# Group normalization on one core: VectorE's scaling in a register loop, and no spacer loads

## The chip, the cores and the metric

The kernel runs on one core of one Trainium2 chip. The metric is the device time in microseconds (us) of one execution. Before the change the median of 3 runs is 633.09 us (632.92 to 633.27). The core has five instruction streams that meet only in semaphores: TensorE (PE in the profile), VectorE (DVE), ScalarE (ACT), GpSimd (POOL) and SyncE (SP), which here only issues DMAs. The DMAs run on 16 DMA engines.

## The reference

The input x has shape (128, 1024, 32, 16) in bfloat16, 134 MB; the output has the same shape. The 1024 channels fall into 32 groups of 32 channels. For each sample and group the mean and variance over 32 channels times 512 pixels (16,384 elements) are taken, and then each channel is scaled and shifted:

```python
xr = x.reshape(B, G, C // G, H, W)
mu = xr.mean(axis=(2, 3, 4), keepdims=True)
var = ((xr - mu) ** 2).mean(axis=(2, 3, 4), keepdims=True)
xn = (xr - mu) / jnp.sqrt(var + 1e-5)
return xn.reshape(B, C, H, W) * g[None, :, None, None] + b[None, :, None, None]
```

With one scale and one bias per (sample, group, channel) this is out = x * (rstd * g) + (b - mean * rstd * g).

## The kernel before

**Tiling.** A tile holds 4 samples times 32 groups on the 128 partitions; each partition has its 32 channels times 512 pixels, so a tile is 128 x 16,384 bfloat16, 4.19 MB, 32 KB of consecutive DRAM per partition. There are 32 tiles and 6 buffers `xt` (NBUF). Tile i lies in buffer (i + 4) % 6. A tile is loaded, worked on in place and stored from the same buffer.

**The stages of one tile.** SP loads it. TensorE adds up its 32 channels into one PSUM bank with 32 matmuls against the identity (L194). VectorE turns the bank into minus the mean with one accumulating pass of 512 elements (`mean`, L211). ScalarE squares the two halves of the tile with that bias and accumulates (L316), then makes the standard deviation (L330, L337). VectorE takes the reciprocal (L223), makes 32 scales (`scl`, L226) and 32 biases (`bia`, L233) and scales the tile, one instruction per channel, 32 of 128 x 512 (L243). The last of them raises `s_dve`, and SP stores the tile (L171).

**The order on VectorE** is the mean of tile i + 1 first, then the reciprocal, scales, biases and 32 scalings of tile i. So the scaling of a tile waits until the next tile has been loaded and summed.

**The loop.** PE, ACT and DVE each run a loop of 6 trips over the 6 buffers, entered at buffer 4 (`loop`, L95). The body of VectorE is written out for all 6 buffers, with constant addresses; at the end of a trip it waits once, sets three semaphore counts back, adds one to the trip's register and branches.

**SP's queue** sets the order of the DMAs. All go through one queue, which the DMA engines take in order. SP first issues 6 loads and one spacer, a load of 128 x 32 elements (64 bytes a partition) into a tile that nobody reads. Then it walks over the tiles: wait for `s_dve`, store. After the stores 1, 4, 7, ... 25 it issues three loads (two after store 1), each behind a wait until the store from that buffer has landed, and one more spacer:

```python
            if (NT - NBUF - 1 - i) % RUN == 0 and i < NT - NBUF:
                for n in range(max(NBUF, i + 1 + NBUF - RUN), min(i + 1 + NBUF, NT)):
                    load(n)
                spacer()
```

So the DMA engines see runs of three stores and three loads, and a spacer after each run of loads. A spacer waits until the spacer before it has landed. The last six stores follow without loads.

The lines below are those of the kernel before.

## Time and profile before

| What | Value |
|---|---|
| time, median of 3 runs | 633.09 us |
| the profiled execution: time / span | 633.13 us / 631.3 us |
| DMA: share of the 16 engines' span, mean rate | 99.0%, 425 GB/s |
| HBM read / written | 134.30 MB / 134.22 MB |
| ACT busy | 476.2 us (75%) |
| DVE busy | 375.8 us (60%), 1024 scalings L243 among 1188 instructions |
| PE busy | 255.1 us (40%) |
| spacers | 10, 8 KB each |

The span goes from the first to the last instruction of the profiled execution; its time is 1.8 us longer. The busy share of an engine is an average over a start, a steady stretch and an end. In the timeline an entry "x32" merges neighbouring instructions: its first number is the start, the second the length of the whole. The bracket behind an entry is the idle time of that engine just before it and what ended it; "issue" means that the profile shows nothing that was waited for. An entry of SPq is the issue of a DMA, not its transfer.

### The profile page before, as it was taken

The page shows a single profiled execution, that of the slowest core. Times are in us where ns is not written, and L with a number is a line of the kernel's source. Part 1 is how long each engine was busy: PE and PEld are TensorE (multiplying, and loading weights), DVE is VectorE, ACT ScalarE, POOL GpSimd, SP SyncE. Part 2 cuts the span into 40 slices and gives each one's busy share as a digit, 9 for nine tenths or more (in the row PEclk, how much of TensorE's full clock was granted, in tenths as well). Part 3 has the DMA queues.
Part 4 walks back from the last instruction along what each step waited for, and adds up shares of the span by engine and source line. Part 5 has one row for each costly group of instructions (what it writes and reads, how often), then busy time and mean ns, then how long its engine had stood idle before and what let it go on. Part 6 is the DMA issues. An engine that isn't in the chain of part 4 may idle for free. (4 is left out here: it accounts for less than half of the span.)

```text
span 631.3 us, 3704 instructions
## 1 busy us (share of the span) xinstructions
PE 255.1 (40%) x1009; PEld 105.4 (17%) x1025; DVE 375.8 (60%) x1188; ACT 476.2 (75%) x194; POOL 0.9 (0%) x7
## 2 busy tenths in 40 slices
PE   0967409009602750582087018404720770095000
PEld 0423103003201320230032003101300230032000
DVE  0057777774772777077727735770777177447771
ACT  0499999995994699189929965993899199649930
POOL 0000000000000000000000000000000000000000
PEclk9998858658855985687578659855975796598555
DMA  8999999999999999999999999999999999999996
GB/s 363 432 432 414 434 432 432 438 432 432 430 432 434 430 430 434 432 430 432 432 432 432 432 432 430 432 432 432 430 432 434 432 430 432 432 432 436 438 394 283
DMA packets 10756, 268.57 MB, mean 425 GB/s; under 512 B 2560, under 2 KB 2560, under 8 KB 2560
## 3 DMA queue, kind: packets, MB, share of 16 engines
q1 hardware_dynamic: 10656, 268.52, 99.0%
q10 hardware_dynamic: 96, 0.00, 0.0%
q14 instruction: 3, 0.02, 0.0%
q8 instruction: 1, 0.02, 0.0%
HBM read 134.30 MB, written 134.22 MB: 425 GB/s over the span
## 5 line engine op out<-in xcount | busy, mean ns | idle before, releaser
L316 ACT ACTIVATE ja<-xt,negmean 128x8192 fp8e5<-128x8192 bf16 x64 | 455.5, 7117 | 126.9 <-DVE jd L211 125.5
L194 PE MATMUL pa<-xt,eye 128*128 128x512 bf16 x1008 | 254.9, 414 | 312.4 <-PEq L192 310.9
L243 DVE TENSOR_SCALAR xt<-xt,scl,bia 128x512 bf16<-128x512 bf16 x1024 | 333.7, 408 | 1.2
L194 PEld LDWEIGHTS pa<-xt,eye 128*128 128x128 bf16 x1024 | 105.3, 105 | 461.6 <-issue 366.0
L211 DVE TENSOR_SCALAR_CACHE_REDUCE jd<-pa 128x512 bf16<-128x512 f32 x33 | 22.7, 687 | 147.3 <-PE pa L194 145.4
L223 DVE RECIPROCAL rstd<-std 128x1 f32<-128x1 f32 x32 | 5.2, 163 | 78.1 <-ACT std L337 78.1
L316 ACT ACTIVATION_READ_ACCUMULATOR ja<-xt,negmean 128x1 f32 x64 | 11.9, 186 | 0.0
L337 ACT ACTIVATE std<-sq,half 128x1 f32<-128x1 f32 x32 | 9.4, 295 | 1.0
L330 ACT ACTIVATE half<-sq,eps_t 128x1 f32<-128x1 f32 x32 | 8.9, 278 | 0.0
L233 DVE SCALAR_TENSOR_TENSOR bia<-scl,negmean,gb 128x32 f32<-128x32 f32 x32 | 8.1, 252 | 1.1
L226 DVE TENSOR_SCALAR scl<-gb,rstd 128x32 f32<-128x32 f32 x32 | 7.7, 241 | 1.1
L262 DVE COPY gb<-gb_p 128x64 f32<-128x64 f32 x1 | 0.2, 226 | 10.7 <-PE gb_p L181 10.7
L181 PE MATMUL gb_p<-gb_b,rep 32*128 32x64 bf16 x1 | 0.2, 231 | 12.5 <-DMA gb_b<-in_b_dram 12.5
L211 DVE DVE_READ_ACCUMULATOR jd<-pa 128x1 f32 x33 | 2.7, 83 | 0.0
L312 ACT ACT_TABLE_LOAD x1 | 1.3, 1283 | 1.9 <-issue 1.9
L181 PEld LDWEIGHTS gb_p<-gb_b,rep 32*128 32x128 bf16 x1 | 0.1, 100 | 12.5 <-DMA gb_b<-in_b_dram 12.5
L261 DVE MEMSET ones_b<- 128x128 bf16 x1 | 0.2, 165 | 1.9 <-issue 1.9
L289 POOL TENSOR_SCALAR_AFFINE_SELECT rep<-ones_b 32x128 bf16<-32x128 bf16 x1 | 0.3, 303 | 0.0
L280 POOL TENSOR_SCALAR_AFFINE_SELECT eye<-ones_b 128x128 bf16<-128x128 bf16 x1 | 0.3, 294 | 1.7 <-DVE ones_b L261 1.7
L312 ACT ACTIVATE warm<-eps_t 128x1 f32<-128x1 f32 x1 | 0.2, 203 | 0.0
L298 POOL TENSOR_SCALAR eps_t<-ones_b 128x1 f32<-128x1 bf16 x1 | 0.2, 205 | 0.0
L378 POOL MEMSET const-uint8-127<- 128x1 uint8 x1 | 0.1, 103 | 0.0
(3 smaller groups left out, 0.3 us busy)
## 6 DMA issues: line engine op xcount, KB each, us to landing
xt<-in_x_dram SPq DMA_DIRECT2D x32, 4096.0 KB, 29.1
out_dram<-xt SPq DMA_DIRECT2D x32, 4096.0 KB, 33.2
spare<-in_x_dram SPq DMA_DIRECT2D x10, 8.0 KB, 29.2
gb_b<-in_g_dram ACTq DMA_DIRECT2D x1, 2.0 KB, 7.8
gb_b<-in_b_dram ACTq DMA_DIRECT2D x1, 2.0 KB, 11.0
```

The lines of the kernel that those rows point to most:

```text
L181: pe.matmul(out=gb_p[:].rearrange("p a k -> p (a k)"), lhsT=rep[:], rhs=gb_b[:].rearrange("q a k -> q (a k)"), start=True, stop=True,).the ...
L194: m = pe.matmul(out=pa[j][:], lhsT=eye[:], rhs=xt[j][:, k * MM_FREE : (k + 1) * MM_FREE], start=(k == 0), stop=(k == NMM - 1),)
L211: dve.tensor_scalar(out=jd[j % 2][:], in0=pa[j % NBUF][:], scalar1=-inv_n, scalar2=None, op0=ALU.mult, op1=ALU.add, accum_out=col(negmean, j),
L223: dve.reciprocal(out=col(rstd, j), in_=col(std, j))._wait_ge(s_std, j + 1).then_inc(s_dd, 1)
L226: dve.tensor_scalar(out=scl[j][:], in0=gam, scalar1=col(rstd, j), scalar2=None, op0=ALU.mult,)._wait_ge(s_dd, 3 * j + 2).then_inc(s_dd, 1)
L233: dve.scalar_tensor_tensor(out=bia[j][:], in0=scl[j][:], scalar=col(negmean, j), in1=bet, op0=ALU.mult, op1=ALU.add,)._wait_ge(s_dd, 3 * j ...
L243: m = dve.tensor_scalar(out=span, in0=span, scalar1=scl[j][:, k : k + 1], scalar2=bia[j][:, k : k + 1], op0=ALU.mult, op1=ALU.add,)
L280: pool.affine_select(out=eye[:], in_=ones_b[:], pattern=[[-1, P]], compare_op=ALU.is_equal, fill=0.0, base=0, channel_multiplier=1,)._wait ...
L312: act.activation(out=warm[:], in_=eps_t[:], func=ACT.Sqrt)
L316: m = act.activation(out=ja[:], in_=xt[j][:, h * F // 2 : (h + 1) * F // 2], func=ACT.Square, bias=col(negmean, j), scale=1.0, accum_out=s ...
L330: act.activation(out=col(half, j), in_=sq[:, 2 * j : 2 * j + 1], func=ACT.Identity, bias=eps_t[:], scale=inv_n,)._wait_ge(s_sq, 3 * j + 1) ...
L337: act.activation(out=col(std, j), in_=sq[:, 2 * j + 1 : 2 * j + 2], func=ACT.Sqrt, bias=col(half, j), scale=inv_n,)._wait_ge(s_sq, 3 * j + ...
```

## The change

It has two parts.

**VectorE's loop.** The body written out for 6 buffers becomes a loop over the 32 tiles with the buffer's number `j` in a register. The six buffers become slices of one tile `x_all`, the PSUM banks slices of `pa_all`, and the addresses come from expressions of registers (`at`, with `bass.ds`). `scl`, `bia` and `rstd` have one copy instead of six. The 32 scalings become an inner loop of 4 rounds of 8 instructions; the addresses of the tile's span, of the scale's column and of the bias's column depend on the round's register `r`, and the span on `j` too. Before the inner loop VectorE waits for the three small instructions (`s_dd` of 3) and sets the count back; after it comes a drain, and the raise of `s_dve` is an instruction of its own instead of riding on the last scaling. The counts of `s_pe`, `s_std` and `s_dd` are set back by separate instructions in each tile instead of once per trip. The broadcast of gamma and beta gets a semaphore of its own (`s_gbp`).

**SP's queue.** The ten spacers, the waits of a spacer for the one before it and the wait for the last one at the kernel's end go. Loads and stores keep their order.

The loops of PE and ACT stay; GpSimd's three set-up instructions are only wrapped in a function. That part of the diff is left out.

```diff
@@ -18,8 +18,8 @@
 NBUF = 6
 RUN = 3
 MM_FREE = 512
+SCALE_STEP = 8
 ENTRY = 4
-SPARE = 32
 
 
 @with_exitstack
@@ -45,7 +45,8 @@
     inv_n = 1.0 / float(F)
     NMM = F // MM_FREE
     TRIPS = (NT + ENTRY) // NBUF
-    assert F % MM_FREE == 0 and NT + ENTRY == TRIPS * NBUF
+    assert KC % SCALE_STEP == 0 and F % MM_FREE == 0
+    assert NT + ENTRY == TRIPS * NBUF
 
     x_v = x.rearrange("(t n) (g k) h w -> t (n g) (k h w)", n=NS, g=G)
     o_v = out.rearrange("(t n) (g k) h w -> t (n g) (k h w)", n=NS, g=G)
@@ -55,14 +56,14 @@
     sb = ctx.enter_context(tc.tile_pool(name="sb", bufs=1))
     ps = ctx.enter_context(tc.tile_pool(name="ps", bufs=1, space=bass.MemoryType.PSUM))
 
-    xt = [sb.tile([P, F], BF16, name=f"xt{j}") for j in range(NBUF)]
+    x_all = sb.tile([P, NBUF * F], BF16, name="x_all")
+    xt = [x_all[:, j * F : (j + 1) * F] for j in range(NBUF)]
     ja = sb.tile([P, F // 2], FP8, name="ja")
     jd = [sb.tile([P, MM_FREE], BF16, name=f"jd{n}") for n in range(2)]
     gb_b = sb.tile([G, 2, KC], BF16, name="gb_b")
     gb = sb.tile([P, 2, KC], F32, name="gb")
     eps_t = sb.tile([P, 1], F32, name="eps_t")
     warm = sb.tile([P, 1], F32, name="warm")
-    spare = sb.tile([P, SPARE], BF16, name="spare")
     ones_b = sb.tile([P, P], BF16, name="ones_b")
     eye = sb.tile([P, P], BF16, name="eye")
     rep = sb.tile([G, P], BF16, name="rep")
@@ -70,10 +71,11 @@
     sq = sb.tile([P, 2 * NBUF], F32, name="sq")
     half = sb.tile([P, NBUF], F32, name="half")
     std = sb.tile([P, NBUF], F32, name="std")
-    rstd = sb.tile([P, NBUF], F32, name="rstd")
-    scl = [sb.tile([P, KC], F32, name=f"scl{j}") for j in range(NBUF)]
-    bia = [sb.tile([P, KC], F32, name=f"bia{j}") for j in range(NBUF)]
-    pa = [ps.tile([P, MM_FREE], F32, name=f"pa{j}") for j in range(NBUF)]
+    rstd = sb.tile([P, 1], F32, name="rstd")
+    scl = sb.tile([P, KC], F32, name="scl")
+    bia = sb.tile([P, KC], F32, name="bia")
+    pa_all = ps.tile([P, NBUF * MM_FREE], F32, name="pa_all")
+    pa = [pa_all[:, j * MM_FREE : (j + 1) * MM_FREE] for j in range(NBUF)]
     gb_p = ps.tile([P, 2, KC], F32, name="gb_p")
 
     def sem(name):
@@ -83,8 +85,8 @@
     st = [sem(f"st{j}") for j in range(NBUF)]
     s_gb, s_set, s_eye, s_rep = sem("s_gb"), sem("s_set"), sem("s_eye"), sem("s_rep")
     s_pe, s_mean, s_sq, s_std = sem("s_pe"), sem("s_mean"), sem("s_sq"), sem("s_std")
-    s_spare = sem("s_spare")
     s_dd, s_dve = sem("s_dd"), sem("s_dve")
+    s_gbp = sem("s_gbp")
 
     def buf(i):
         return (i + ENTRY) % NBUF
@@ -145,17 +147,7 @@
                 set_up()
         nc.switch_bb(end)
 
-    spacers = [0]
-
     def sync_program(sync):
-        def spacer():
-
-            n = spacers[0]
-            spacers[0] += 1
-            if n:
-                sync.wait_ge(s_spare, 16 * n)
-            sync.dma_start(out=spare[:], in_=x_v[0][:, 0:SPARE]).then_inc(s_spare, 16)
-
         def load(i):
             j = buf(i)
             if i >= NBUF:
@@ -164,7 +156,6 @@
 
         for i in range(min(NBUF, NT)):
             load(i)
-        spacer()
         for i in range(NT):
             j = buf(i)
             sync.wait_ge(s_dve, i + 1)
@@ -172,8 +163,7 @@
             if (NT - NBUF - 1 - i) % RUN == 0 and i < NT - NBUF:
                 for n in range(max(NBUF, i + 1 + NBUF - RUN), min(i + 1 + NBUF, NT)):
                     load(n)
-                spacer()
-
+        
     def tensor_program(pe):
         def prepare():
             pe.wait_ge(s_gb, 32)
@@ -184,7 +174,7 @@
                 rhs=gb_b[:].rearrange("q a k -> q (a k)"),
                 start=True,
                 stop=True,
-            ).then_inc(s_pe, 1)
+            ).then_inc(s_gbp, 1)
             pe.wait_ge(s_eye, 1)
 
         def step(j):
@@ -205,103 +195,97 @@
         pe.sem_inc(s_pe, 1)
 
     def vector_program(dve):
+        es = bass.OrderedEngineSet([dve.engine])
         gam, bet = gb[:, 0, :], gb[:, 1, :]
 
-        def mean(j):
+        def at(t, j, n):
+            return t[:, bass.ds(j * n, n)]
+
+        def mean(j, n=0):
             dve.tensor_scalar(
-                out=jd[j % 2][:],
-                in0=pa[j % NBUF][:],
+                out=jd[n][:],
+                in0=at(pa_all, j, MM_FREE),
                 scalar1=-inv_n,
                 scalar2=None,
                 op0=ALU.mult,
                 op1=ALU.add,
-                accum_out=col(negmean, j),
-            )._wait_ge(s_pe, j + 2).then_inc(s_mean, 1)
-
-        def step(j):
-            mean(j + 1)
-            dve.reciprocal(out=col(rstd, j), in_=col(std, j))._wait_ge(
-                s_std, j + 1
-            ).then_inc(s_dd, 1)
+                accum_out=at(negmean, j, 1),
+            )._wait_ge(s_pe, 1).then_inc(s_mean, 1)
+            dve.sem_inc(s_pe, -1)
+
+        dve.memset(ones_b[:], 1.0).then_inc(s_set, 1)
+        dve.tensor_copy(out=gb[:], in_=gb_p[:])._wait_ge(s_gbp, 1).then_inc(s_dd, 1)
+        dve.wait_ge(s_dd, 1)
+        dve.sem_inc(s_dd, -1)
+        mean(ENTRY, 1)
+        with nc.Fori(ENTRY, NT + ENTRY, 1, engines=es) as i:
+            j = i % NBUF
+            mean((i + 1) % NBUF)
+            dve.reciprocal(out=rstd[:], in_=at(std, j, 1))._wait_ge(s_std, 1).then_inc(
+                s_dd, 1
+            )
+            dve.sem_inc(s_std, -1)
             dve.tensor_scalar(
-                out=scl[j][:],
+                out=scl[:],
                 in0=gam,
-                scalar1=col(rstd, j),
+                scalar1=rstd[:],
                 scalar2=None,
                 op0=ALU.mult,
-            )._wait_ge(s_dd, 3 * j + 2).then_inc(s_dd, 1)
+            )._wait_ge(s_dd, 1).then_inc(s_dd, 1)
             dve.scalar_tensor_tensor(
-                out=bia[j][:],
-                in0=scl[j][:],
-                scalar=col(negmean, j),
+                out=bia[:],
+                in0=scl[:],
+                scalar=at(negmean, j, 1),
                 in1=bet,
                 op0=ALU.mult,
                 op1=ALU.add,
-            )._wait_ge(s_dd, 3 * j + 3).then_inc(s_dd, 1)
-            for k in range(KC):
-                span = xt[j][:, k * HW : (k + 1) * HW]
-                m = dve.tensor_scalar(
-                    out=span,
-                    in0=span,
-                    scalar1=scl[j][:, k : k + 1],
-                    scalar2=bia[j][:, k : k + 1],
-                    op0=ALU.mult,
-                    op1=ALU.add,
-                )
-                if k == 0:
-                    m._wait_ge(s_dd, 3 * j + 4)
-                if k == KC - 2 and j == NBUF - 1:
-                    m.then_inc(s_dd, 1)
-            m.then_inc(s_dve, 1)
-
-        def settle():
-            dve.wait_ge(s_dd, 3 * NBUF + 2)
-
+            )._wait_ge(s_dd, 2).then_inc(s_dd, 1)
+            dve.wait_ge(s_dd, 3)
+            dve.sem_inc(s_dd, -3)
+            with nc.Fori(0, KC // SCALE_STEP, 1, engines=es) as r:
+                for n in range(SCALE_STEP):
+                    k = r * SCALE_STEP + n
+                    span = at(x_all, j * KC + k, HW)
+                    dve.tensor_scalar(
+                        out=span,
+                        in0=span,
+                        scalar1=at(scl, k, 1),
+                        scalar2=at(bia, k, 1),
+                        op0=ALU.mult,
+                        op1=ALU.add,
+                    )
+            dve.drain()
+            dve.sem_inc(s_dve, 1)
+
+    def pool_program(pool):
         def prepare():
-            dve.memset(ones_b[:], 1.0).then_inc(s_set, 1)
-            dve.tensor_copy(out=gb[:], in_=gb_p[:])._wait_ge(s_pe, 1).then_inc(s_dd, 1)
-            dve.sem_inc(s_pe, ENTRY)
-            mean(ENTRY)
-
-        loop(
-            dve,
-            prepare,
-            step,
-            settle,
-            [
-                (s_pe, NBUF, 0),
-                (s_std, NBUF, ENTRY),
-                (s_dd, 3 * NBUF + 1, 3 * ENTRY),
-            ],
-            ahead=True,
-        )
-
...
     def scalar_program(act):
         act.dma_start(out=gb_b[:, 0, :], in_=g_v).then_inc(s_gb, 16)
@@ -358,7 +342,6 @@
             block.gpsimd(pool_program)
             block.scalar(scalar_program)
 
-        nc.sync.wait_ge(s_spare, 16 * spacers[0])
         for j in range(NBUF):
             nc.sync.wait_ge(st[j], 16 * sum(buf(i) == j for i in range(NT)))
 
```

More of the change, by code (lines that the diff above doesn't have):

```diff
@@ L279, in pool_program @@
-    def pool_program(pool):
-        pool.affine_select(
-            out=eye[:],
-            in_=ones_b[:],
-            pattern=[[-1, P]],
-            compare_op=ALU.is_equal,
-            fill=0.0,
-            base=0,
-            channel_multiplier=1,
-        )._wait_ge(s_set, 1).then_inc(s_eye, 1)
-        pool.affine_select(
-            out=rep[:].rearrange("q (n a) -> q n a", n=NS),
-            in_=ones_b[0:G, :].rearrange("q (n a) -> q n a", n=NS),
-            pattern=[[0, NS], [-1, G]],
-            compare_op=ALU.is_equal,
-            fill=0.0,
-            base=0,
-            channel_multiplier=1,
-        ).then_inc(s_rep, 1)
-        pool.tensor_scalar(
-            out=eps_t[:],
-            in0=ones_b[:, 0:1],
-            scalar1=EPS,
-            scalar2=None,
-            op0=ALU.mult,
-        ).then_inc(s_set, 1)
+            )._wait_ge(s_dd, 2).then_inc(s_dd, 1)
@@ new lines, in vector_program @@
+            dve.drain()
+            dve.sem_inc(s_dve, 1)
+    def pool_program(pool):
+        def prepare():
+            pool.affine_select(
+                out=eye[:],
+                in_=ones_b[:],
+                pattern=[[-1, P]],
+                compare_op=ALU.is_equal,
+                fill=0.0,
+                base=0,
+                channel_multiplier=1,
+            )._wait_ge(s_set, 1).then_inc(s_eye, 1)
+            pool.affine_select(
+                out=rep[:].rearrange("q (n a) -> q n a", n=NS),
+                in_=ones_b[0:G, :].rearrange("q (n a) -> q n a", n=NS),
+                pattern=[[0, NS], [-1, G]],
+                compare_op=ALU.is_equal,
+                fill=0.0,
+                base=0,
+                channel_multiplier=1,
+            ).then_inc(s_rep, 1)
+            pool.tensor_scalar(
+                out=eps_t[:],
+                in0=ones_b[:, 0:1],
+                scalar1=EPS,
+                scalar2=None,
+                op0=ALU.mult,
+            ).then_inc(s_set, 1)
+        prepare()
```

## The prediction

> **What bounds the kernel now.** I read the page's slices and DMA queues first, then the timeline of SP's queue, then the DVE timeline at a trip's end and over the last tiles.
>
> ```profile
> span 631.3 us, 3704 instructions
> ...
> DMA  8999999999999999999999999999999999999996
> ...
> q1 hardware_dynamic: 10656, 268.52, 99.0%
> ```
>
> The 16 DMA engines are busy from the first slice to the last but one. Only at the two ends can other work set the time. One period of SP's and PE's timeline:
>
> ```profile
> 171.67 19.68 SPq L163 DMA_DIRECT2D xt<-in_x_dram  x3
> 191.40 0.43 SPq L157 DMA_DIRECT2D spare<-in_x_dram  x1
> 191.87 29.63 SPq L171 DMA_DIRECT2D out_dram<-xt  x3
> ...
> 200.83 1.44 PE L194 MATMUL pa<-xt,eye 128*128 128x512 bf16 x3 [30.03 <-PEq L192]
> 210.53 7.07 PE L194 MATMUL pa<-xt,eye 128*128 128x512 bf16 x31 [1.23 <-PEq L192]
> 220.61 8.75 PE L194 MATMUL pa<-xt,eye 128*128 128x512 bf16 x32 [3.01 <-PEq L192]
> ...
> 230.22 19.68 SPq L163 DMA_DIRECT2D xt<-in_x_dram  x3
> ```
>
> A load is issued when the store from its buffer has landed, so the three loads from 171.67 give three store landings 9.68 us apart: the last issue ends at 171.67 + 19.68 = 191.35 and lasts 0.33, so it began at 191.02, and (191.02 - 171.67)/2 = 9.68. PE starts when a load lands: 200.83, 210.53, 220.61. The next store lands at 230.22. The steps are 9.81 (store to load), 9.70 (load to load), 10.08, 9.61. The period is 58.55 us; over the seven from the SP issue at 113.18 to that at 522.64 the mean is 58.49, so 19.50 us per tile. The last store of this batch was issued at 191.87 + 29.63 = 221.50 at the latest; its turn came one step before it landed at 249.58, at 239.9. So in the steady part VectorE has 18 us to spare. The end has none:
>
> ```profile
> 572.34 0.68 DVE L211 TENSOR_SCALAR_CACHE_REDUCE jd<-pa 128x512 bf16<-128x512 f32 x1
> ...
> 587.47 0.68 DVE L211 TENSOR_SCALAR_CACHE_REDUCE jd<-pa 128x512 bf16<-128x512 f32 x1
> ...
> 591.09 7.11 ACT L316 ACTIVATE ja<-xt,negmean 128x8192 fp8e5<-128x8192 bf16 x1
> ...
> 606.09 0.16 DVE L223 RECIPROCAL rstd<-std 128x1 f32<-128x1 f32 x1 [3.07 <-ACT std L337]
> ...
> 606.85 10.43 DVE L243 TENSOR_SCALAR xt<-xt,scl,bia 128x512 bf16<-128x512 bf16 x32
> 617.30 0.33 SPq L171 DMA_DIRECT2D out_dram<-xt  x1
> ...
> 617.00:618.00 1.00, 0.00 (x0) 0.00 (x0) 0.28 (x1) 0.00 (x0) 0.00 (x0) 0.50 0.23 98
> 618.00:620.00 2.00, 0.00 (x0) 0.00 (x0) 0.00 (x0) 0.00 (x0) 0.00 (x0) 0.50 1.12 475
> ```
>
> After the last run of loads the last four tiles follow each other through ScalarE (14.87 us a tile) and VectorE. The last tile's 32 scalings take 10.43 us, its store is issued at 617.30, and the DMA engines, down to a share of 0.23 by then, have only that store left (last number but one of a window: DMA share). So an added microsecond in the last tile's scaling is a microsecond of the kernel.
>
> **Part 1: VectorE's loop.** One scaling is 407 ns long by the line's row, but 32 take 10.43, so they start (10.43 - 0.41)/31 = 0.323 us apart; that pace is the engine's. The change adds sequencer work per scaling: the instruction's own slot and, since the span, the scale's column and the bias's column all move with the round's register, at least three address additions unless constants are folded. No row shows a register instruction alone. Two rows bound its price. From above, VectorE's own trip end:
>
> ```profile
> 163.25 0.69 DVE L211 TENSOR_SCALAR_CACHE_REDUCE jd<-pa 128x512 bf16<-128x512 f32 x1 [0.39 <-issue]
> ...
> 55.16 7.12 ACT L316 ACTIVATE ja<-xt,negmean 128x8192 fp8e5<-128x8192 bf16 x1 [0.33 <-ACTq L349]
> ```
>
> There a wait (released by the 31st scaling, 0.32 before the 32nd ends), three count changes, an addition, a branch and the mean's own slot pass in 0.32 + 0.39 = 0.71 us: at most 0.10 us each. From the other side, ACT's trip end has a drain, two count changes, an addition and a branch in 0.33 us, 0.066 each, part of which is the drain. I take 0.06 to 0.10 as the range and 0.09 as value, close to VectorE's own row.
>
> At 0.09 a scaling has four slots, 0.36 us, more than 0.323: 32 x 0.037 = 1.2 us a tile. Each of the 4 rounds closes with an addition, a compare-and-branch, its jump and a new base, 4 slots: 4 x 4 x 0.09 = 1.4 us, uncovered since the sequencer has no lead. Ahead of the loop come a wait, a count change, a move, a jump and a base (5 slots, 0.45), behind it a drain and the raise (2 slots, 0.18); before, the first scaling started 0.03 us behind the biases and the raise rode on the last. So a tile's scaling grows by d = 1.2 + 1.4 + 0.45 + 0.18 = 3.3 us.
>
> In the steady part that is hidden: 10.43 + 3.3 + 1.5 (mean 0.69, its read-out 0.08, 0.16, 0.24, 0.25 and gaps) is 15.2 of the 19.50 us that the DMAs need; that cover is gone only above (19.50 - 1.5 - 0.6)/32 = 0.54 us per scaling. At the end one d shows in full. What is late next: the mean of tile 30 ends at 573.0 and ScalarE takes it at 576.2; that of 31 ends at 588.1 and is taken at 591.1. Beyond about 3.1 us of d the mean stands behind the scaling of the tile before and VectorE sets the pace alone: from its release at 560.6 by the last but two load (mean 0.6, small instructions 0.8, four scaling blocks B, three times 1.4 between) the last scaling ends at 566.2 + 4B, against 606.85 + B while ScalarE leads; these cross at B = 13.55. So the end moves by d up to 3.1 and by four times the rest: 3.1 + 4 x 0.2 = **+3.9 us**. With 0.06 a slot the engine's pace stays: four slots are 0.24, the lead of 8 x 0.08 us covers a round's closing, and d is 7 x 0.06 = 0.4. With 0.10 d is 2.5 + 1.6 + 0.7 = 4.8 and the end moves by 9.9.
>
> The counts set back per tile (`s_pe`, `s_std`) lie in VectorE's idle time behind the mean (3.07 us before the reciprocal). The single `scl`, `bia` and `rstd` cost nothing beyond the drain already counted. The start is covered: the second store is issued at 66.09 and its turn comes at 74.36.
>
> **Part 2: the spacers.** On SP a spacer costs 0.43 us of issue in front of a store that was free to go, but the queue ahead is two loads deep (29.2 us from issue to landing), so that is hidden: nothing. On the DMA engines the turn from loads to stores, spacer included, is 58.49 - 9.81 - 9.70 - 2 x 9.68 = 19.62 for two steps, 0.24 more than 9.70 + 9.68. That bounds the gain: nothing of it, or all. Below nothing too: a turn without spacer occurs nowhere. The nearest row is the other turn, store to load, which has no spacer and costs 9.81 - 9.69 = 0.12. I take 0.24 - 0.12 = 0.12 gained; nine spacers lie ahead of the load that releases the last tiles (551.81): **-1.1 us**, at most -2.2. The last wait on `s_spare` was long over: nothing.
>
> A rule that would make this much larger: the Trainium skill's "DMA: Bandwidth & Descriptors" (Rules for kernel authors) says that transfers under 64 KB are mostly overhead, and its section on latency gives a fixed cost of about 2 us; an estimate by that page is 10 x 2 = 20 us gained, where the trace leaves room for 0.24 us each, since transfers queue up behind each other.
>
> **Sum.** The profiled execution is 633.13 us (631.3 of span and 1.8 around it), 0.04 above the median: 633.1 + 3.9 - 1.1 = **635.9 us**, with 633.8 (0.08 a slot: d = 1.8) to 641.9 (0.10) as this case's own range.
>
> **Rivals.** *Faster: VectorE's sequencer runs ahead and the spacers pay in full.* For it: ACT's 0.066 us. Against it: every tile empties VectorE's queue first. Time: 633.1 + 0.4 - 2.2 = 631.3. It decides at about 0.075 us a slot: below that, rounds close under the lead; above, the end loses more than the spacers give.
>
> *The same pace, spacers half paid.* 633.1 + 0.4 - 1.1 = 632.4, within 0.2%. The Trainium skill's "Runtime: NRT & Kernel Launch" (Instruction fetch mechanics) speaks for this one: a floor of about 20 cycles per instruction, which at the 0.96 GHz of "Advanced Engine Details and Errata" (Clock Domains) is an estimate of 0.02 us a slot, by which the sum would be near 632.1; VectorE's 0.71 us for seven slots doesn't show so low a price.
>
> *Slower by much: addresses worked out anew for every scaling.* Multiplications by 512 and 32, the sums and three bases make some 8 register instructions, with its own slot 9; even at 0.06 that is 0.54 us a scaling. d = 32 x 0.217 + 4 x 0.24 + 0.4 = 8.3, the end moves by 3.1 + 4 x 5.2 = 24; with 8 slots (0.48) d = 6.4 and 16. Less 1.1: 648 to 656. Against it: constants may be folded into fewer additions.
>
> *The turn from loads to stores is dearer without a spacer.* The one loose row is the first turn: the sixth load lands 64.74 - 53.88 = 10.86 us after the fifth, 1.15 over its step. If each turn lost 0.35 instead of gaining, 633.1 + 3.9 + 3.2 = 640. Against it: the other turn costs 0.12.
>
> **Numbers.** Chances: my forecast 0.35, the faster rival 0.17, the same pace 0.11, anew 0.25, dearer turn 0.12. The range 631 to 651 leaves out the top of "anew" and a corner of "faster". Less than 0.2% (1.3 us) can hardly be told from no change: faster 0.19, same 0.14, slower 0.67 (the forecast's low end counts partly as same).
>
> **What would show it.** DVE's row for L243 with idle time by "issue" inside the 32, 32 of them taking 13 to 14 us; first scaling about 0.45 us behind the biases; the last store issued 2 to 3 us later than 617.30; the DMA slices as full as before; landings at the loads-to-stores turn 9.7 to 9.8 apart. Wrong if 32 scalings still take 10.5 us, if they take 15 or more, or if the period is not 58.3 to 58.5.

## The result and the profile after

The changed kernel takes 637.58 us (median of 4 runs, 637.02 to 638.21) against 633.00 us (4 runs, 632.88 to 633.27) in the same session. The ratio is 1.0068, 95% interval 1.0055 to 1.0080: slower by 0.7%, which is 4.3 us by the ratio and 4.6 by the medians. The forecast was 635.9 us and slower. The total lies only 1.7 us above it, but that is luck: the term for the loop was 2.1 us too large, and the steady part, from which a gain of 1.1 was forecast, lost 2.4.

The page of the changed kernel, its head, its DMA slices and its main queue:

```profile
span 635.4 us, 6308 instructions
...
DMA  8999999999999999999999999999999999999966
...
q1 hardware_dynamic: 9216, 268.44, 98.2%
```

The slices read as before except for the last but one, which falls from 9 to 6; the forecast was that all would stay as full. The full ones can't show what happened: a slice of 15.9 us reads 9 from 90% on. The number of instructions went from 3704 to 6308, and that turns out to matter. The engine's own work is still 1188 instructions on VectorE. The rest is what its sequencer executes for the loops: in the trace's records VectorE has 3857 entries instead of 1243, among them 67 fused register instructions, 6 additions and 5 compare-and-branches for each tile.

The timeline of VectorE (start, length, instruction, idle time before it) from the mean of tile 29 on, which runs ahead of the scaling of tile 28:

```profile
563.87 0.69 DVE L205 TENSOR_SCALAR_CACHE_REDUCE jd<-pa_all 128x512 bf16 x1 [16.62 <-PE pa_all L184]
...
564.96 0.25 DVE L235 SCALAR_TENSOR_TENSOR bia<-scl,negmean,gb 128x32 f32<-128x32 f32 x1
565.77 2.75 DVE L249 TENSOR_SCALAR x_all<-x_all,scl,bia  x8 [0.56 <-DVEq L244]
568.76 2.74 DVE L249 TENSOR_SCALAR x_all<-x_all,scl,bia  x8 [0.23 <-issue]
571.72 2.74 DVE L249 TENSOR_SCALAR x_all<-x_all,scl,bia  x8 [0.23 <-issue]
574.69 2.74 DVE L249 TENSOR_SCALAR x_all<-x_all,scl,bia  x8 [0.23 <-issue]
578.09 0.69 DVE L205 TENSOR_SCALAR_CACHE_REDUCE jd<-pa_all 128x512 bf16 x1 [0.66 <-issue]
...
593.22 0.69 DVE L205 TENSOR_SCALAR_CACHE_REDUCE jd<-pa_all 128x512 bf16 x1 [0.66 <-issue]
...
610.63 2.75 DVE L249 TENSOR_SCALAR x_all<-x_all,scl,bia  x8 [0.56 <-DVEq L244]
...
619.55 2.74 DVE L249 TENSOR_SCALAR x_all<-x_all,scl,bia  x8 [0.23 <-issue]
```

The loop's cost can be read in the brackets. The 32 scalings go from 565.77 to 574.69 + 2.74 = 577.43, 11.66 us instead of 10.43. Within a round they start (2.74 - 0.41)/7 = 0.333 us apart instead of 0.323. Rounds start 2.97 apart, 0.30 more than 8 x 0.333; the engine stands idle for 0.23 of it. The entry, with its wait, costs 0.56 of idle time instead of 0.03. The store of the last tile is issued 0.06 behind the last scaling instead of 0.02. So one tile's scaling grows by 1.23 + 0.53 + 0.04 = 1.80 us.

When ScalarE takes the mean of tiles 30 and 31 (two of its rows; between them the second half of the same tile is left out):

```profile
579.49 7.11 ACT L300 ACTIVATE ja<-x_all,negmean 128x8192 fp8e5<-128x8192 bf16 x1
...
594.36 7.11 ACT L300 ACTIVATE ja<-x_all,negmean 128x8192 fp8e5<-128x8192 bf16 x1
```

The means end at 578.8 and 593.9 with their read-outs, 0.7 and 0.4 us ahead of ScalarE, where it was about 3 us before. ScalarE still sets the pace of the last tiles, 14.87 us each.

Now the steady part: SP's queue in one early period and at the end, and TensorE's first sum behind the last but two load.

```profile
171.72 19.68 SPq L155 DMA_DIRECT2D x_all<-in_x_dram  x3
191.44 32.21 SPq L162 DMA_DIRECT2D out_dram<-x_all  x3
...
465.74 20.08 SPq L155 DMA_DIRECT2D x_all<-in_x_dram  x3
485.86 31.78 SPq L162 DMA_DIRECT2D out_dram<-x_all  x3
524.63 20.12 SPq L155 DMA_DIRECT2D x_all<-in_x_dram  x3
544.79 77.89 SPq L162 DMA_DIRECT2D out_dram<-x_all  x6
```

```profile
554.24 1.44 PE L184 MATMUL pa_all<-x_all,eye 128*128 128x512 bf16 x3 [30.78 <-PEq L182]
```

The late rows of the kernel before:

```profile
464.00 19.68 SPq L163 DMA_DIRECT2D xt<-in_x_dram  x3
...
522.64 19.67 SPq L163 DMA_DIRECT2D xt<-in_x_dram  x3
```

```profile
551.81 1.44 PE L194 MATMUL pa<-xt,eye 128*128 128x512 bf16 x3 [31.78 <-PEq L192]
```

Each of the three loads is issued when a store has landed, so stores land (length - 0.33)/2 apart. At 171.72 that is (19.68 - 0.33)/2 = 9.68 us, as before. At 465.74 it is 9.88, at 524.63 9.90. Before, it was 9.67 to 9.68 to the end. A period grows by less than three slower stores would make it: by the completion records (they are explained behind e5), from 280 us on, the steps to the second and third store of a run are 0.21 us longer than before and the step to the first 0.27, but the third load lands 9.69 behind the second instead of 9.99. The last period is 524.63 - 465.74 = 58.89 where it was 522.64 - 464.00 = 58.64. Over the seven periods from 113 us on, the sum is 411.08 us against 409.46. The other loads are still 9.70 apart.

The difference of the two spans, 635.4 - 631.3 = 4.1 us, closes like this:

| stretch | before | after | difference |
|---|---|---|---|
| start to landing of the last but two load (TensorE starts) | 551.81 | 554.24 | +2.43 |
| landing to the mean of that tile | 8.80 | 9.63 | +0.83 |
| mean to the end of the last scaling | 56.67 | 58.42 | +1.75 |
| last scaling to the issue of the last store | 0.02 | 0.06 | +0.04 |
| issue of the last store to the end of the span | 14.00 | 13.05 | -0.95 |

VectorE's loop at the end is worth 1.8 us. The larger part, 2.4 us, comes from the steady part, where nothing was forecast but a small gain. The two other rows nearly cancel. The 0.83 is TensorE's: the 32 matmuls of that sum took from 8.5 to 9.9 us over the runs below, in kernels with the same matmuls, under a granted clock that changes from slice to slice (5 to 9 tenths in the page's slices). I take it for scatter. The -0.95 is taken up behind e5, where the DMA engines are looked at one by one.

So the question for the experiments was: which part of the change makes the stores of the steady part slower?

### The profile page after: what moved, and what is told of

Read it like the earlier page. It is cut to its first block, busy times and chain, and to the rows that moved or that the text cites. A ratio compares the mean times of both kernels' runs of the same rounds, so it can differ in the third digit from the quotient of the medians.

```text
span 635.4 us, 6308 instructions
## 1 busy us (share of the span) xinstructions
PE 257.9 (41%) x1009; PEld 105.9 (17%) x1025; DVE 394.8 (62%) x1188; ACT 476.2 (75%) x194; POOL 0.9 (0%) x7
## 2 busy tenths in 40 slices
DMA packets 9314, 268.47 MB, mean 423 GB/s; under 512 B 1120, under 2 KB 1120, under 8 KB 1120
## 5 line engine op out<-in xcount | busy, mean ns | idle before, releaser
L300 ACT ACTIVATE ja<-x_all,negmean 128x8192 fp8e5<-128x8192 bf16 x64 | 455.5, 7117 | 130.2 <-DVE jd L205 128.8
L184 PE MATMUL pa_all<-x_all,eye 128*128 128x512 bf16 x1008 | 257.7, 417 | 311.9 <-PEq L182 310.1
L249 DVE TENSOR_SCALAR x_all<-x_all,scl,bia x1024 | 351.0, 412 | 40.0 <-issue 22.1
L184 PEld LDWEIGHTS pa_all<-x_all,eye 128*128 128x128 bf16 x1024 | 105.8, 105 | 463.3 <-issue 369.4
L205 DVE TENSOR_SCALAR_CACHE_REDUCE jd<-pa_all 128x512 bf16 (+1 forms) x33 | 22.8, 692 | 149.5 <-PE pa_all L184 134.3
L224 DVE RECIPROCAL rstd<-std 128x1 f32 x32 | 5.2, 162 | 23.3 <-ACT std L321 23.3
L300 ACT ACTIVATION_READ_ACCUMULATOR ja<-x_all,negmean 128x1 f32 x64 | 11.9, 186 | 0.0
L205 DVE DVE_READ_ACCUMULATOR jd<-pa_all (+1 forms) x33 | 2.7, 83 | 0.0
```

The costliest lines, as they stand in the source:

```text
L184: m = pe.matmul(out=pa[j][:], lhsT=eye[:], rhs=xt[j][:, k * MM_FREE : (k + 1) * MM_FREE], start=(k == 0), stop=(k == NMM - 1),)
L205: dve.tensor_scalar(out=jd[n][:], in0=at(pa_all, j, MM_FREE), scalar1=-inv_n, scalar2=None, op0=ALU.mult, op1=ALU.add, accum_out=at(negmea ...
L224: dve.reciprocal(out=rstd[:], in_=at(std, j, 1))._wait_ge(s_std, 1).then_inc(s_dd, 1)
L249: dve.tensor_scalar(out=span, in0=span, scalar1=at(scl, k, 1), scalar2=at(bia, k, 1), op0=ALU.mult, op1=ALU.add,)
L300: m = act.activation(out=ja[:], in_=xt[j][:, h * F // 2 : (h + 1) * F // 2], func=ACT.Square, bias=col(negmean, j), scale=1.0, accum_out=s ...
```

## The experiments

The theories, by the letters of the expectations: A, the spacers kept the stores quick, and without them the stores slow down, which is close to the rival of the dearer turn; B, the slower stores come from VectorE's loop or from the one big tile `x_all`, and the spacers' gain is as predicted; C, which came when the store spacing was read, it is the number of executed instructions, whichever engine executes them; D, it is VectorE's own loop, its register addresses or its later stores.

**e1, only the spacers go.** The kernel before with the three spacer pieces taken out of SP's program.

```diff
         for i in range(min(NBUF, NT)):
             load(i)
-        spacer()
...
                     load(n)
-                spacer()
...
-        nc.sync.wait_ge(s_spare, 16 * spacers[0])
```

> Part 2 alone: the kernel before, with the ten spacers and their waits taken out and VectorE's code untouched. The changed kernel's last-but-two load landed at 554.24 us instead of 551.81, and its three stores of a run landed 9.88 us apart instead of 9.68. Theory A (the spacers keep the stores quick, whatever VectorE does): this kernel shows stores 9.85 to 9.9 apart, a period of 58.8 to 58.9 us and a time 2 to 3 us above before, 635 to 636. Theory B (my prediction; the slower stores come from VectorE's loop or from the one big tile): the period stays at 58.3 to 58.5 and the time is 632 to 633.

Measured: 633.66 us (11 runs) against 633.41 (20 runs), ratio 1.0004, 0.9995 to 1.0013. In microseconds that is +0.25, between -0.3 and +0.8. The last two periods of its SP timeline:

```profile
464.49 19.67 SPq L163 DMA_DIRECT2D xt<-in_x_dram  x3
...
522.94 19.69 SPq L163 DMA_DIRECT2D xt<-in_x_dram  x3
```

The period is 58.45 and the stores are 9.67 to 9.68 apart. The last but two load lands at 552.12 (551.81 before). Ten loads of 8 KB, queued among transfers of 4 MB, cost nothing that can be measured, and so their removal gains nothing. A falls; so does the dearer turn. The period is as B had it, but the gain that would have brought the time to 632 or 633 is not there. The span is even 0.5 us longer (631.8 us); where that lies is shown behind e5.

**e2, only the loop.** The changed kernel with the spacers put back where they were.

```diff
+        spacer()
...
+                spacer()
...
+        nc.sync.wait_ge(s_spare, 16 * spacers[0])
```

> Part 1 alone: the changed kernel with the ten spacers put back. VectorE's block of 32 scalings takes 11.66 us instead of 10.43 in the changed kernel's trace, and starts 0.53 us later behind the biases, so 1.8 us at the end. Theory A (the spacers keep the stores quick): stores 9.68 apart, period 58.5, time 1.8 us above before, 634.8, up to 635.6 if the sum of the first of the last tiles again falls on a slow clock (0.8 us). Theory B (VectorE's loop slows the stores): stores 9.88 apart, period 58.9, time as the changed kernel's, 637.5.

Measured: 637.54 us (5 runs), ratio 1.0070, 1.0056 to 1.0084: the whole difference. From its SP timeline:

```profile
466.38 20.09 SPq L166 DMA_DIRECT2D x_all<-in_x_dram  x3
...
525.33 20.11 SPq L166 DMA_DIRECT2D x_all<-in_x_dram  x3
```

The stores are (20.09 - 0.33)/2 = 9.88 apart, with spacers in place. So the loop on VectorE, or the one tile `x_all` that came with it, makes the stores slower, though neither changes what the DMA queue is given. The tile is not needed for it: e4, e4b and e6 below keep six separate buffers and have slower stores.

**e3, one round of 32.** The changed kernel with the inner loop running once, so all columns of scale and bias are constants and no round closes.

```diff
-SCALE_STEP = 8
+SCALE_STEP = 32
```

> The changed kernel with one round of 32 scalings instead of four of 8: only the rounds' closing goes, three gaps of 0.23 us and the rounds' starts. If a round's closing costs what its gap shows and the pace in a round (0.333 us) is the engine's, the block of 32 falls from 11.66 to about 10.5 us and the time by 1.1 to 1.2 us against the changed kernel, 636.4. If instead the register work sets the pace, the block stays at 10.7 or more and the time falls by less than 1 us.

Measured: 634.87 us (10 runs), ratio 1.0024, 1.0015 to 1.0034; 2.7 us less than the changed kernel, where 1.1 to 1.2 was expected. Its page's head, its SP queue late and the last block of scalings:

```profile
span 633.3 us, 5092 instructions
```

```profile
523.64 19.98 SPq L155 DMA_DIRECT2D x_all<-in_x_dram  x3
```

```profile
608.13 10.42 DVE L249 TENSOR_SCALAR x_all<-x_all,scl,bia  x32 [0.33 <-DVEq L244]
```

The block is back at 10.42 us. With one fused register instruction per scaling instead of two (1120 in all instead of 2144), the pace is the engine's 0.323. The issue of the last store comes 3.74 us earlier than in the changed kernel: 1.24 are the block and 0.2 the entry, 1.15 a shorter first sum (8.49 us), which is scatter, and 1.14 come from ahead of that, since the last but two load lands at 553.10 instead of 554.24. Not all of the 3.74 reaches the time, since a late DMA engine ends this kernel (the second table behind e5). With 1216 instructions fewer, its stores are 9.82 apart late in the run instead of 9.88. That put theory C on the table in numbers.

**e4 and e4b, an idle loop on GpSimd.** The kernel before; GpSimd, which has nothing to do after set-up, runs an empty loop. Nothing waits for it, and it touches no data. e4b has four drains in each iteration.

```diff
+        idle = bass.OrderedEngineSet([pool.engine])
+        with nc.Fori(0, 1300, 1, engines=idle):
+            pass
```

```diff
+        idle = bass.OrderedEngineSet([pool.engine])
+        with nc.Fori(0, 1300, 1, engines=idle):
+            for _ in range(4):
+                pool.drain(fusable=False)
```

> The kernel before, with an empty loop of 1300 iterations (an addition and a branch each, 2600 sequencer instructions) on GpSimd behind its set-up; GpSimd has nothing else to do and nobody waits for the loop. VectorE's code is that of before. What is to be told apart: why three stores of a run land 9.88 us apart in the changed kernel from about 290 us on instead of 9.68, while one DMA engine of the 16 falls back by 0.2 us with every store (7.8 us behind the middle one at 534 us, 4.7 in the kernel before). Theory C (it is the number of executed instructions, 6308 against 3704, whichever engine executes them, as if each left something behind that the slow DMA engine has to share its way to memory with): with 6300 instructions this kernel shows stores 9.8 to 9.9 apart while the loop runs, and its time is 1 to 2.5 us above before, though VectorE is untouched. Theory D (it is VectorE's own loop, its register addresses or its later stores): stores stay 9.68 apart, time as before within 0.5 us.

> The same with four drains in each of the 1300 iterations on GpSimd: 7800 instructions more than before. Theory C: the stores slow down further than in the loop without drains while it runs, to 10 us or more apart, and the time is 2 to 6 us above before. Theory D: nothing moves, stores 9.68 apart, time as before.

Measured: e4 635.37 us (5 runs), ratio 1.0036, 1.0022 to 1.0051; e4b 641.82 us (4 runs), ratio 1.0140, 1.0123 to 1.0157. Two rows of e4:

```profile
230.71 20.27 SPq L163 DMA_DIRECT2D xt<-in_x_dram  x3
...
289.86 19.84 SPq L163 DMA_DIRECT2D xt<-in_x_dram  x3
```

The head of e4b's page, its SP timeline late in the run, and its last block of scalings:

```profile
span 639.7 us, 11521 instructions
```

```profile
350.22 20.44 SPq L163 DMA_DIRECT2D xt<-in_x_dram  x3
...
528.74 20.47 SPq L163 DMA_DIRECT2D xt<-in_x_dram  x3
```

```profile
613.92 10.43 DVE L243 TENSOR_SCALAR xt<-xt,scl,bia 128x512 bf16<-128x512 bf16 x32
```

This is the plainest run of the study. VectorE's block is untouched at 10.43 us, SP's program is untouched, and the kernel is 8.8 us slower (2 to 6 were expected) because another engine goes through an empty loop 1300 times. The stores are 10.06 us apart and the last but two load lands at 558.68, 6.87 later. In e4 the loop ended at 284.8 us: its stores reach 9.97 apart in the period that begins at 230.71, while the loop runs, and fall back to 9.76 behind it. Theory D, by which the stores stay 9.68 apart in both, falls.

**e5, half of TensorE's sums.** The changed kernel with every second matmul of a sum left out. This was to tell whether instructions of any engine count.

```diff
-            for k in range(NMM):
+            for k in range(0, NMM, 2):
...
-                    stop=(k == NMM - 1),
+                    stop=(k == NMM - 2),
```

> The changed kernel with every second matmul left out: the means are sums over 16 of the 32 channels, so this part of the computation is missing. 1024 instructions on TensorE (512 matmuls, 512 weight loads) fewer, 5280 in all. Theory C: the stores come out 9.82 to 9.85 apart, as in the kernel with one round of 32, which executes 5092; the last load but two lands 0.5 to 1.2 us earlier than 554.2. Theory D: stores stay 9.88 apart, that load lands at 554. The sums of a tile are ready about 3.5 to 4.5 us sooner either way, so the time falls by 4 us or so under D and by 4.5 to 5.5 under C.

Measured: 636.53 us (4 runs), ratio 1.0051, 1.0034 to 1.0068. Its head, its SP queue late, and its last scalings:

```profile
span 634.7 us, 5300 instructions
```

```profile
465.83 20.09 SPq L155 DMA_DIRECT2D x_all<-in_x_dram  x3
```

```profile
615.13 2.74 DVE L249 TENSOR_SCALAR x_all<-x_all,scl,bia  x8 [0.23 <-issue]
```

With a thousand instructions fewer than the changed kernel, all of them TensorE's (two records for a matmul), the stores are as slow: 9.88 apart, here from the first period on, and the last but two load lands at 554.26 (554.24). So theory C as stated, whichever engine executes them, is wrong for TensorE. There is a second lesson. The sums are shorter, so the last scaling ends at 617.87, 4.4 us earlier than in the changed kernel, and yet the time is only 1.05 us lower, where both theories expected 4 us or more. Something other than the chain of the last tiles must set the end here.

**What ends late: some of the 16 DMA engines.** Each DMA of 4.19 MB leaves 16 completion records in the trace; I read them as one for each DMA engine. Sorted by time, and taken from the fifth of the 16, the last three of a DMA came this much later (us; the DMA that landed near the time given):

| kernel | 172 us | 291 to 299 us | 495 to 504 us |
|---|---|---|---|
| before | 1.1, 2.5, 2.8 | 2.3, 3.3, 3.4 | 3.9, 4.2, 4.5 |
| e6 (below) | 2.1, 2.6, 3.4 | 3.3, 3.8, 3.9 | 4.2, 4.8, 6.1 |
| changed | 0.4, 2.4, 3.1 | 0.5, 3.8, 4.3 | 0.5, 5.2, 7.1 |
| e5 | 0.5, 0.6, 2.0 | 0.7, 0.9, 4.6 | 1.7, 2.5, 7.1 |
| e4b | 2.5, 2.7, 2.8 | 3.1, 3.4, 5.4 | 3.9, 4.2, 10.4 |

In every kernel some engines fall behind slowly, the third latest by 0.5 to 4.2 us at 500 us. One goes further where more instructions are executed. The trace does not name the engines, but the packets show that it is one alone. A packet of 32 KB takes 1.213 us nearly everywhere. Those that take longer between 465 and 485 us, 16 of them in the changed kernel (1.227 to 1.260 us) and 16 in e4b (1.246 to 1.284), each begin within 4 ns of the end of the one before: two stores' packets, eight each, of one engine. In the kernel before there are 14 such packets, of 1.215 to 1.242 us. A store has landed only when its latest engine is done, and the next load waits for that. Between the last two columns a period adds (7.1 - 4.3)/3.33 = 0.84 us of lag in the changed kernel, (10.4 - 5.4)/3.50 = 1.43 in e4b, (6.1 - 3.9)/3.50 = 0.63 in e6 and 1.1/3.50 = 0.31 in the kernel before, at about 390, 910, 390 and 148 executed instructions a period on the engines other than TensorE. For an instruction that is (1.43 - 0.84)/520 = 1.1 ns, (0.63 - 0.31)/242 = 1.3, (1.43 - 0.31)/762 = 1.5 or (0.84 - 0.31)/242 = 2.2 ns: an estimate of one to two ns, no better, since the engine that is the latest at 300 us need not be the one that is the latest at 500.

The same records show what ends each kernel (us):

| kernel | issue of the last store | most engines end it | last engine ends the store before | last engine ends it |
|---|---|---|---|---|
| before | 617.30 | 628.27 | 619.57 | 629.81 |
| e5 | 617.93 | 628.89 | 623.06 | 632.68 |
| e3 | 618.61 | 629.58 | 621.67 | 631.35 |
| e6 (below) | 620.23 | 631.19 | 622.27 | 632.50 |
| changed | 622.35 | 633.31 | 623.13 | 633.42 |
| e4b | 624.38 | 635.35 | 628.01 | 638.25 |

Most engines end the last store 10.96 or 10.97 us behind its issue. The latest ones were still busy with the store before. So the end is the later of two chains: ScalarE and VectorE's plus 10.96, and the latest engine's. In the kernel before it was already the engine's, by 629.81 - 628.27 = 1.5 us. In the changed kernel both end together. That is the row of -0.95 above: this wait of 1.4 to 1.5 us is gone, and 0.5 us more follow behind the last landing (span less landing: 1.49 before, 1.99 after). In e5 VectorE's chain is 4.4 us earlier, and the engine ends the kernel at 632.68. In e3 it ends it 1.8 us behind the rest.

The 0.5 us come with the spacers' removal. All five traced kernels with spacers (before, e2, e4, e4b, e6) end 1.49 us behind the last landing, all five without them (changed, e1, e3, e5, e7) 1.99. It lies on SP: its closing drain starts 0.98 us behind the last landing instead of 0.61 and takes 0.13 instead of 0.007. Why is not shown.

**e6 and e7, the same number of instructions without VectorE's loop.** e6 is the kernel before, where GpSimd runs 38 empty iterations for each tile, released by TensorE: as many instructions as the changed kernel executes, spread in the same way, with VectorE as it was. e7 is the changed kernel again, beside it on the same chip.

```diff
+            pe.sem_inc(s_pool, 1)
...
+        with nc.Fori(0, NT, 1, engines=idle):
+            pool.wait_ge(s_pool, 1)
+            pool.sem_inc(s_pool, -1)
+            with nc.Fori(0, 38, 1, engines=idle):
+                pass
```

> The kernel before with the changed kernel's extra instructions moved to GpSimd: after each tile's sums TensorE raises a count, GpSimd waits for it and runs an empty loop of 38 iterations, about 80 instructions a tile, where the changed kernel's VectorE executes 81 more a tile. VectorE's code is that of before. Revised theory (each instruction that VectorE or GpSimd executes sets one DMA engine back by a little over 1 ns, TensorE's do not; the stores slow down once this engine is the last one): stores of a run 9.85 to 9.9 apart from about 290 us on, the last load but two lands at 553.5 to 554.5 us, VectorE's last block still takes 10.43 us, and the time is 2 to 2.6 us above before, which leaves about 2 us of the change for VectorE's tail. Rival (the stores slow down because of what VectorE's loop does to its own scalings and stores, and the earlier loop on GpSimd did something else): stores 9.68 apart, time within 0.7 us of before.

> The changed kernel as it is, timed beside the one above. Its time less that of the kernel with the same count on GpSimd is what VectorE's loop costs at the end alone: 1.8 us by its trace (1.23 us longer block, 0.53 us later start, 0.04 us later raise), 1.5 to 2.5 with the clock of the first sum and the start of the last store; under the rival of the other run it is the whole 4 to 4.5 us.

Measured: before 633.22 us (9 runs); e6 635.82 (5 runs, 635.61 to 635.95), ratio 1.0040, 1.0027 to 1.0054; e7 637.42 (5 runs, 636.93 to 637.93), ratio 1.0065, 1.0051 to 1.0078. From e6:

```profile
span 634.0 us, 6297 instructions
```

```profile
465.41 19.88 SPq L163 DMA_DIRECT2D xt<-in_x_dram  x3
...
524.21 19.95 SPq L163 DMA_DIRECT2D xt<-in_x_dram  x3
```

```profile
609.78 10.42 DVE L244 TENSOR_SCALAR xt<-xt,scl,bia 128x512 bf16<-128x512 bf16 x32
```

And from e7:

```profile
524.54 20.12 SPq L155 DMA_DIRECT2D x_all<-in_x_dram  x3
```

The stores of e6 are 9.78 to 9.81 apart late in the run (9.90 in e7; 9.85 to 9.9 was expected of e6), and its last but two load lands at 553.64 (554.13 in e7). Its time is as expected. This splits the change in two: 635.82 - 633.22 = 2.60 us come with the instructions alone, without VectorE's loop, `x_all` or a missing spacer, and 637.42 - 635.82 = 1.60 us are what is left to the rest of the change. By the completions e6 still ends with the latest engine (632.50, most engines at 631.19) and e7 with VectorE's chain (633.6): VectorE's own 1.8 us are seen only in so far as they reach beyond the engine, 1.1 us here, and 0.5 are the longer rest behind the last landing, which belongs to the spacers. Why the stores of e7 are still 0.1 us further apart than e6's at the same count is open. No run was faster than the kernel before beyond the measurement; e1 equals it.

All kernels in one table, by instructions executed:

| kernel | instructions | last but two load lands | time |
|---|---|---|---|
| e1 | 3694 | 552.12 | 633.66 |
| before | 3704 | 551.81 | 633.0 to 633.4 |
| e3 | 5092 | 553.10 | 634.87 |
| e5 (TensorE's halved) | 5300 | 554.26 | 636.53 |
| e6 | 6297 | 553.64 | 635.82 |
| changed, e7 | 6308 | 554.24, 554.13 | 637.58, 637.42 |
| e2 | 6318 | 554.93 | 637.54 |
| e4 (loop ends early) | 6321 | 553.58 | 635.37 |
| e4b | 11521 | 558.68 | 641.82 |

Leaving out e5, whose missing instructions were TensorE's, the landing moves by 0.7 to 1.2 ns for each instruction more than before: (554.24 - 551.81)/2604 = 0.93, (558.68 - 551.81)/7817 = 0.88, e6 0.71, e2 1.19.

**What stays open.** Why an executed instruction costs a DMA engine one to two ns is not settled. Every run here has a span and a clock listed and so was recorded by the hardware profiler; whether the records are what loads that engine, or something else, and so whether an unrecorded execution has the same loss, no run tells. The fetching of instructions by DMA doesn't show as the cause: the pages list 4 packets on the instruction queues before, 2 in the changed kernel and 4 in e4b. The stores become slow from about 240 us on in the changed kernel and 350 in e6, but from the first period in e5 and from 171 us in e4b. The reason is argued, not shown: in the other traces of this table one engine is already 1.4 to 2.0 us behind by 54 us and covers the lagging one until that overtakes it; in e5 all engines were within 0.5 us at that time, and nothing covers it. Why those others lag is open too.

## Why the prediction was right in its total and wrong in its parts

**The price of a slot and of a round's closing (failed, mis-sized).** The step put four slots of 0.09 us on a scaling, 0.36 us, hence 1.2 us a tile. There are three (two fused register instructions and the scaling), and the pace is 0.333, hence 32 x 0.010 = 0.3 us. The closing of a round was put at 0.36, four times 1.4 us; it is 0.30, an addition and a compare-and-branch, and only three of them lie inside the block: 0.9 us. The entry was well sized (0.45; 0.53 measured), the raise was not (0.18; 0.04). The sum d is 1.80 us instead of 3.3. At 0.08 a slot the prediction's working gives 1.8 as well, but by chance: it has no cost within a round there. The 32 scalings take 11.66 us where the prediction had 13 to 14.

On the rule that was weighed there: the Trainium skill's "Runtime: NRT & Kernel Launch" (Instruction fetch mechanics) gave, by the estimate in the prediction, 0.02 us a slot. As a price the runs don't bear that out, though a floor may lie below what is paid: three slots would then take 0.06 and hide under 0.323, and a closing would be 0.04. With one register instruction the pace is the engine's, with two it is 0.333, so a slot costs at most about 0.11 us, and the closing shows that it is not far below. GpSimd's empty loop in e4 takes 0.217 us a round for the same two instructions, an addition and a compare-and-branch.

**"What is late next" (mechanism not reached).** The step said that beyond about 3.1 us of d the mean would stand behind the scaling of the tile before and VectorE would set the pace alone, which made 3.3 into 3.9. The margin shrank faster than described: the mean of tile 30 starts 14.22 us behind that of tile 29 instead of 11.73, 2.5 us for a d of 1.8, because it also stands 0.66 behind the last scaling of its trip. ScalarE takes it 0.7 us after it is ready instead of 3. With d at 1.8 the kink is not reached, and the chain moves by d, 1.75 us.

**"An added microsecond in the last tile's scaling is a microsecond of the kernel" (failed).** The step read a DMA share of 0.23 at 617 to 618 us as engines that have only the last store left. But 0.23 of 16 is three to four engines still at work on the store before: the completions show three of them finishing the store before at 619.41 to 619.57; they ended the last one 0.8 to 1.5 us behind the rest. So in the kernel before, the chain of the last tiles had 1.5 us to spare, and the first 1.5 of any delay at the end would have been free. In the changed kernel this cover had been used up by the slower stores and the longer first sum, which moved the same chain by 3.3 us.

**"In the steady part that is hidden" (failed).** The working compared VectorE's busy time with the 19.50 us that the DMAs need for a tile. That comparison was right and VectorE never is late there. What it left out is that the DMAs' own time is no constant: the sequencer's additional instructions alone make it longer. e6 has VectorE's old program and loses 2.60 us, and the changed kernel's last but two load lands 2.43 us later. Both bounds of the price of this edit were drawn from VectorE's rows; none was drawn for what the engine's instructions do to the DMAs, and the prediction's own sign of error, a period outside 58.3 to 58.5, is what came: 58.7 in the mean of the seven, 58.9 at the end. Two more of its signs failed with it: the last store is issued 5.0 us later, not 2 to 3, and the first store of a run lands 10.05 behind the last load, not 9.7 to 9.8.

**Part 2, the spacers (failed).** The step took -1.1 us. e1 shows +0.25, between -0.3 and +0.8. The 0.24 us by which the turn from loads to stores was dearer than two plain steps is not the spacer's: the mean period is 58.49 us with spacers and 58.49 without (e1). The reading took the landing of loads from TensorE's start, some 0.13 us later; by the completions the turn from stores to loads costs nothing, and what is dearer is mainly the third load, 9.99 behind the second before and 10.08 in e1. The term that was put at nothing, the end without the last wait, costs the 0.5 us behind the last landing. On the opposite side, the Trainium skill's "DMA: Bandwidth & Descriptors" (Rules for kernel authors), by which transfers of 8 KB would be mostly overhead, is not borne out for small transfers that lie in a queue of large ones; the prediction's estimate from that page was 20 us for the ten. The trace's bound of 0.24 us each was the right kind of argument; the measured gain was at its lower end.

**The sum.** The forecast was 633.1 + 3.9 - 1.1 = 635.9. Measured against the profiled execution: the chain's last store is issued 2.43 (steady part) + 0.83 (the first sum) + 1.79 (VectorE's loop) = 5.05 us later; less 1.4 for the late engines that had ended the kernel before, plus 0.5 behind the last landing (the spacers' removal) and 0.1 around the span, that is 633.1 + 4.2 = 637.3. A term for the loop that was too large by 2.1 and 1.5 us of cover that was overlooked stood against a gain of 1.1 that didn't exist and 2.4 (steady part), 0.8 (first sum) and 0.5 us (end) that were missing. That they nearly cancel is luck. Of the rivals, "addresses worked out anew" was wrong by the count of instructions: constants were folded into one or two fused ones. "Sequencer runs ahead" was right on the pace within a round to 0.01 us, and wrong at each round's closing and entry, where nothing is covered. The dearer turn is excluded by e1.

## What to carry to other kernels

In a kernel that keeps the DMA engines busy throughout, ask not only whether an engine has time to spare, but also how many instructions its sequencer executes: in these recorded runs 2600 more on GpSimd cost 2.4 to 2.6 us although nothing waited for them. Read a full DMA row by the spacing of landings and by the 16 completions of each DMA, at the end of the kernel above all: a slice of the page reads 9 either way, and a late engine can be what ends the kernel while a compute chain looks as if it did. VectorE's loop is paid above all at its entry and at each closing of a round, where the engine stands idle, so fewer and longer rounds (e3) save more than the pace within a round suggests.

## What the runs showed of the hardware that was not expected

- One of the 16 DMA engines falls behind the others in stores by an estimated one to two ns for each instruction executed on VectorE or GpSimd; 1008 fewer records of TensorE made no difference (stores 9.88 us apart with and without them). An empty loop with drains on GpSimd (7800 instructions) made the kernel 1.4% slower.
- Ten queued loads of 8 KB cost nothing measurable (+0.25 us for taking them out, between -0.3 and +0.8).
- Loop costs on VectorE: one fused register instruction per 0.323 us scaling is hidden, two give 0.333; a closing of a round adds 0.30 us, entering behind a wait on the engine's own last result 0.53; behind a round's last scaling with a drain and a raise, the next instruction starts 0.66 later.
- In the kernel before, three of the 16 DMA engines lag by 3.9 to 4.5 us at 500 us and end the last store 0.8 to 1.5 us behind the others.
- Without the spacers the span ends 1.99 us behind the last landing instead of 1.49, in five traces against five.
- The first sum of a loaded tile, the same 32 matmuls, took from 8.5 to 9.9 us between runs.
